# An attention kernel with two mixtures of experts: one attention step moved ahead of another, in one place

## The chip, the cores and the metric

The kernel runs on one core of one Trainium2 chip. What counts is the device time of one execution in microseconds. A core has TensorE (matmuls), VectorE, ScalarE, GpSimd (the profile calls it POOL) and SyncE (SP), which issues most of the DMA transfers. Each engine works through its own instructions in the order in which the program gave them, and waits at an instruction until what it needs is there.

## What is computed

A gated linear attention over 4 batches, 8 heads, 768 tokens and 48 numbers a head, then two layers of experts over the 3072 tokens. The attention keeps a state of 48 by 48 numbers for each head:

```python
for t in range(S):
    state = alpha[:, :, t, :, None] * state + np.einsum('bhd,bhe->bhde', k[:, :, t], v[:, :, t])
    y[:, :, t] = np.einsum('bhd,bhde->bhe', q[:, :, t], state)
```

Its result, 3072 rows of 384, goes through 8 experts, all of them for every row, weighted by a matrix P that is normalised eight times by rows and columns; then through 8 other experts of which each row uses two:

```python
for e in range(E):
    h = np.maximum(x @ w1[e], 0.0)
    ye = h @ w2[e]
    out += P[:, e:e + 1] * ye
```

## The kernel before

The 3072 rows are 24 tiles of 128. The attention works in 24 units, one for each tile, counted from 0 as in the code (a unit is one batch and a stretch of 128 tokens). float32 numbers are split into a float16 upper and a float16 lower half, and a product is made of three float16 products; so most steps have an instruction on ScalarE for the upper half and one on VectorE for the lower half, in that order.

A unit i has these steps, each a function that issues instructions on several engines:

- p1(i): two scans and products with k and q on VectorE (L433 to L438), the halves of v (ScalarE L449, VectorE L450), from unit 4 on products for the state on GpSimd (L444).
- p2(i): TensorE turns k (L457) and multiplies k with q (L467); ScalarE (L459) and VectorE (L460) write the turned k in halves, named `ktok`; ScalarE copies the products (L469) and GpSimd masks them (L470).
- p2b(i): the masked products in halves, named `am`: the upper on ScalarE (L477), the lower on VectorE (L478).
- p3(i): TensorE multiplies `am` with v (L491) and `ktok` with v (L498), VectorE writes the state (L504, later L502), ScalarE the result y (L506).
- p4(i): TensorE turns y (L515), ScalarE writes the upper half `xh` of the tile (L517) and VectorE the lower half `xl` (L518).
- p5(i): small products with the gate weights (L526, L527), their sum on VectorE (L531).

While the attention runs, TensorE is also given work of the first expert, as a stream in a fixed order. `g1t(T, w, j)` is a quarter of the hidden layer for w tiles from tile T on (called a hidden unit below): 18 matmuls from `xh`, `xl` and the split weights (L225), a Relu on ScalarE (L229) and the lower half on VectorE (L230), into `hid`. `g2` is the second layer for one tile: 24 matmuls of 384 columns (L238) and a copy on VectorE (L250). A hidden unit needs `xh` and `xl` of all its tiles.

The order of all this is written by one loop. `order_of(i)` lists which step of which unit comes next in round i: p1 of unit i, p3 of i - 2, p2 and p2b of i - 1, p4 of i - 2, p5 of i - 3. After each step the loop adds a fixed cost for it (`TA`: p1 1.5, p2 2.3, p3 1.6, p4 0.5, p5 0.3) to `t_att`, but only once a tile is available, which is the case from the step after p4 of the first unit on. Then it issues stream items, each with its own cost, until their sum reaches 0.8 of `t_att`. So the place of p4(0) decides from which step on costs are counted.

`W0AT` names the steps after which one of the seven weight pieces of the first expert is split (`w0_step`, ScalarE L150 and VectorE L153): three pieces of 128 x 1024 for the first layer, all of which the first hidden unit needs, and four of 128 x 768. Splitting a piece also issues the load of the piece three further on, on SP. The gate weights are split behind p2(1) (L413, L414).

Of the kernel before, what the change touches and what calls it, by code (L numbers as in the profile page):

```python
# [27 lines left out]
RATIO = 0.8  # L28
FINE = (1, 2, 2, 2)
LATE = 4  # L30
W0AT = (("p1", 2), ("p3", 0), ("p4", 0), ("p5", 0), ("p3", 1), ("p2", 2), ("p4", 1))

WR = 4.0
GW = 1.2
# [4 lines left out]


def order_of(i):
    if i < LATE:
        return ("p1", 0), ("load", -3), ("p3", 2), ("p2", 1), ("p4", 2), ("p2b", 1), ("p5", 3)
    return ("p1", 0), ("load", -3), ("p3", 2), ("p2", 1), ("p2b", 1), ("p4", 2), ("p5", 3)
# [3 lines left out]
def kernel(ctx, tc, q, k, v, alpha, w_gate, w1a, w2a, g2w, n2w, noise, w1b, w2b, out):  # L48
# [485 lines left out]
    def att_units():  # L534
        for i in range(NT + 3):
            for n, d in order_of(i):
                f = dict(p1=p1, load=load, p2=p2, p2b=p2b, p3=p3, p4=p4, p5=p5)[n]
                if 0 <= i - d < NT and (n != "load" or i - d >= NL):
                    yield (lambda f=f, j=i - d: f(j)), n, i - d
# [471 lines left out]
    def w0_step():  # L1011
        i = ws0[0]
        if i < NW:
            w_split(0, i, w0.pop(0))
            if i + 3 < NW:
                w0.append(w0_load(i + 3))
            ws0[0] += 1
# [41 lines left out]
    for u, kind, idx in list(att_units()):  # L1059
        u()  # L1060
        if (kind, idx) in W0AT:
            w0_step()
# [320 lines left out]
```

## Time and profile before

| | us |
|---|---|
| median of 3 runs | 2044.93 (2043.68 to 2045.04) |
| the profiled execution | 2044.31 |
| its span, first to last instruction | 2042.6 |
| TensorE busy | 1982.2 |
| VectorE busy | 1247.5 |
| ScalarE busy | 684.7 |
| GpSimd busy | 605.9 |

The attention fills about the first 241 us of the span, with the first expert's stream in between; then come the other experts of the first layer (to about 1560 us), the routing of the second, and its experts. In the rows below a time is us from the start of the span; in a timeline a row is one instruction or several alike (x22), with its start, its duration, what it writes and reads, and in brackets how long the engine stood idle before it and for what it waited (`DVE am L478` is VectorE's instruction of line 478 that writes `am`). The granted clock of TensorE is given as a share of 2.4 GHz; 0.50 is 1.2 GHz.

### The profile page before, as it was taken

Reading aid. Unit: us, or ns where it says so; the run is one execution under the profiler, and the core shown is the slowest. Engines: PE = TensorE matmul, PEld = TensorE weight load, DVE = VectorE, ACT = ScalarE, POOL = GpSimd, SP = SyncE. Lnnn points to the kernel's source line nnn. Section 1 sums busy time; section 2 is a strip of 40 time slices with the busy share of each in tenths; the row PEclk is TensorE's granted clock in tenths of the full one; section 3 lists DMA queues with packets and bytes.
Section 4 is the critical chain, followed back from the end, with each engine's and each line's share of the span. In section 5 each row is a group of like instructions: output and inputs, shape, how many; then the busy total and the mean of one; then the engine's idle time right before and its main releaser. Section 6 shows DMA issues by size and latency. Waiting matters only on the chain. (4 is left out here: it accounts for less than half of the span.)

```text
span 2042.6 us, 37845 instructions
## 1 busy us (share of the span) xinstructions
PE 1982.2 (97%) x15715; PEld 1335.8 (65%) x15715; DVE 1247.5 (61%) x2642; ACT 684.7 (34%) x1338; POOL 605.9 (30%) x452
## 2 busy tenths in 40 slices
PE   6999999999999999999999999999999899999997
PEld 5888756667667766776677677666555455555554
DVE  8889675666666666566656657554335646454441
ACT  5555422333433343234333323332222323222220
POOL 2434212332332343233324322321000243333322
PEclk9999999999999999999999999999999999999999
DMA  6333010000000000000000001003422458465541
GB/s 218 99 99 118 22 42 32 16 17 22 19 17 30 11 17 27 12 27 16 22 12 24 19 12 42 1 1 96 136 70 66 105 105 191 102 126 133 124 72 24
DMA packets 113565, 119.59 MB, mean 59 GB/s; under 512 B 62692, under 2 KB 95741, under 8 KB 113392
## 3 DMA queue, kind: packets, MB, share of 16 engines
q1 hardware_dynamic: 101968, 97.74, 16.8%
q0 software_dynamic: 11136, 18.89, 5.3%
q8 instruction: 124, 2.03, 0.4%
q10 hardware_dynamic: 288, 0.52, 0.1%
q14 instruction: 49, 0.40, 0.1%
HBM read 85.17 MB, written 21.63 MB: 52 GB/s over the span
## 5 line engine op out<-in xcount | busy, mean ns | idle before, releaser
L285 PE MATMUL bank<-xh,wt 128*128 128x512 f16 x1728 | 520.0, 379 | 1.6 <-DVE acc L248 1.6
L304 POOL TENSOR_TENSOR hid<-ss,hid 128x1024 f16<-128x1024 f32 x144 | 306.8, 2131 | 701.6 <-ACT hid L303 658.4
L319 PE MATMUL long<-wt,hid 128*128 128x192 f16 x6048 | 505.7, 246 | 3.5 <-DVE acc L329 2.6
L319 PEld LDWEIGHTS <-hid 128*128 128x128 f16 x6048 | 500.1, 98 | 12.8 <-issue 3.2
L285 PEld LDWEIGHTS <-wt 128*128 128x128 f16 x2592 | 253.1, 98 | 299.1 <-issue 2.0
L238 PE MATMUL bank<-wt,hid 128*128 128x384 f16 (+1 forms) x2496 | 424.5, 327 | 0.1
L238 PEld LDWEIGHTS <-hid 128*128 128x128 f16 (+1 forms) x2496 | 243.9, 99 | 161.1 <-issue 3.7
L285 PE MATMUL bank<-xl,wt 128*128 128x512 f16 x864 | 327.5, 379 | 0.0
L329 DVE SCALAR_TENSOR_TENSOR acc<-long,Pm,acc 128x192 f32<-128x192 f32 (+1 forms) x360 | 187.4, 533 | 148.3 <-PE long L319 147.7
L308 DVE SCALAR_TENSOR_TENSOR hid<-bank,hid 128x256 f16<-128x256 f32 (+1 forms) x288 | 158.8, 552 | 185.9 <-ACT ss L292 185.9
L308 DVE SCALAR_TENSOR_TENSOR ss<-bank,ss 128x256 f32<-128x256 f32 x576 | 240.5, 420 | 48.2 <-ACT hid L297 31.2
L303 ACT ACTIVATE hid<-ss 128x1024 f16<-128x1024 f32 x144 | 152.2, 1057 | 231.6 <-DVE ss L308 231.6
L291 ACT ACTIVATE hid<-bank 128x256 f16<-128x256 f32 x144 | 53.2, 370 | 408.7 <-PE bank L285 408.7
L153 DVE SCALAR_TENSOR_TENSOR wt<-wst,wt 128x384 f16<-128x384 f32 (+2 forms) x216 | 176.1, 825 | 1.8 <-ACT wt L150 1.8
L891 PEld LDWEIGHTS <-wt 128*128 128x128 f16 x1152 | 112.7, 99 | 90.5 <-issue 4.4
L904 POOL DMA_INDIRECT out_dram<-acc,ix x56 | 91.4, 1632 | 257.0 <-DVE acc L903 238.9
L895 DVE SCALAR_TENSOR_TENSOR hid<-bank,hid 128x384 f16<-128x384 f32 (+1 forms) x128 | 74.2, 588 | 119.5 <-ACT hid L894 119.5
L894 ACT ACTIVATE hid<-bank 128x384 f16<-128x384 f32 (+1 forms) x128 | 65.2, 515 | 221.5 <-PE bank L891 221.5
L150 ACT ACTIVATE wt<-wst 128x384 f16<-128x384 f32 (+2 forms) x216 | 109.7, 535 | 76.5 <-DMA wst<-in_moe_w_dram 76.5
L207 PE MATMUL bank<-xh,wt 128*128 128x512 f16 x384 | 121.8, 379 | 0.7 <-DVE acc L329 0.7
L891 PE MATMUL bank<-xl,wt 128*128 128x384 f16 (+1 forms) x576 | 106.5, 342 | 0.0
L891 PE MATMUL bank<-xh,wt 128*128 128x384 f16 (+1 forms) x576 | 106.3, 342 | 0.0
(187 smaller groups left out, 1676.1 us busy)
## 6 DMA issues: line engine op xcount, KB each, us to landing
wst<-in_moe_w_dram SPq DMA_DIRECT2D x38, 512.0 KB, 3.4
wst<-in_moe_w_dram SPq DMA_DIRECT2D x46, 384.0 KB, 3.2
acc<-in_moe_w_dram SPq DMA_DIRECT2D x18, 384.0 KB, 4.6
la<-in_alpha_dram SPq DMA_DIRECT2D x24, 260.0 KB, 2.7
lk<-in_k_dram SPq DMA_DIRECT2D x24, 256.0 KB, 3.0
wt<-in_q_dram SPq DMA_DIRECT2D x22, 256.0 KB, 3.9
acc<-in_moe_w_dram SPq DMA_DIRECT2D x10, 512.0 KB, 7.1
out_dram<-zero SPq DMA_DIRECT2D x6, 768.0 KB, 4.7
```

The source lines that it names most:

```text
L150: nc.scalar.activation(hi, src, AF.Copy, scale=SW)
L153: nc.vector.scalar_tensor_tensor(lo, src, SW, hi, op0=OP.mult, op1=OP.subtract)
L207: nc.tensor.matmul(p, w1s(e, a, kc, f), x[:, kc, s], start=(n == 0), stop=(n == 3 * KC - 1))
L238: nc.tensor.matmul(p, h(a, f, s), w2s(x, b, f), start=(f + n == 0), stop=(f == FC - 1 and n == 2))
L285: nc.tensor.matmul(p, w1s(e, a, kc, f), x[:, kc, tok], start=(n == 0), stop=(n == 3 * KC - 1))
L303: nc.scalar.activation(lefts(e, nb, j, 0, S1, 4), sums, AF.Copy)
L304: nc.gpsimd.tensor_sub(lefts(e, nb, j, 1, S1, 4), sums, lefts(e, nb, j, 0, S1, 4))
L308: nc.vector.scalar_tensor_tensor(out, p, 0.0, x, op0=OP.max, op1=op)
L319: nc.tensor.matmul(out, left(e, nb, j, a, aop)[:, q * 128:(q + 1) * 128], w2t(e, b, wop, j), start=start and n == 0, stop=stop and n == 3 ...
L329: nc.vector.scalar_tensor_tensor(a, p, Pm[:, T, e:e + 1], a, op0=OP.mult, op1=OP.add)
L891: nc.tensor.matmul(p, w1s(x, a, kc, f), xt[:, b * KC + kc, :], start=(i == 0), stop=(i == 3 * KC - 1))
L904: d = nc.gpsimd.indirect_dma_start(out=out, out_offset=bass.IndirectOffsetOnAxis(ap=ix, axis=0), in_=y, in_offset=None, bounds_check=N - 1 ...
```

## The change

In round 2 alone p4(0) is issued ahead of p2(1) in place of behind it. The weight pieces 1 and 2 are split behind p4(0) and p2(1), which before were split behind p3(0) and p4(0); pieces 3 to 6 keep their steps. Nothing else is edited, and no work is added or removed; two new lines shift the line numbers behind them by 2.

```diff
--- before.py
+++ after.py
@@ -28,7 +28,7 @@
 RATIO = 0.8
 FINE = (1, 2, 2, 2)
 LATE = 4
-W0AT = (("p1", 2), ("p3", 0), ("p4", 0), ("p5", 0), ("p3", 1), ("p2", 2), ("p4", 1))
+W0AT = (("p1", 2), ("p4", 0), ("p2", 1), ("p5", 0), ("p3", 1), ("p2", 2), ("p4", 1))
 
 WR = 4.0
 GW = 1.2
@@ -39,6 +39,8 @@
 
 
 def order_of(i):
+    if i == 2:
+        return ("p1", 0), ("load", -3), ("p3", 2), ("p4", 2), ("p2", 1), ("p2b", 1), ("p5", 3)
     if i < LATE:
         return ("p1", 0), ("load", -3), ("p3", 2), ("p2", 1), ("p4", 2), ("p2b", 1), ("p5", 3)
     return ("p1", 0), ("load", -3), ("p3", 2), ("p2", 1), ("p2b", 1), ("p4", 2), ("p5", 3)
```

What the loop makes of it reaches further: a tile counts as available one step earlier, p2(1)'s cost of 2.3 is counted, and from there to the end of the attention the stream items stand some 1.8 (0.8 of 2.3) earlier in the order. 54 items are issued by the end of the attention, 53 before. The order of SP's transfers is the same.

VectorE, at the start, from the copy of unit 0's state on; before:

```order
L504 COPY acc<-bank 128x384
L153 SCALAR_TENSOR_TENSOR wt_72<-acc,wt_72 128x1024
L460 SCALAR_TENSOR_TENSOR ktok<-bank,ktok 128x512
L413 TENSOR_SCALAR wg_111<-wg 128x3x8
L414 SCALAR_TENSOR_TENSOR wg_111<-wg,wg_111 128x3x8
L518 TENSOR_TENSOR xl<-bank,xh 128x3x128
L153 SCALAR_TENSOR_TENSOR wt_72<-acc,wt_72 128x1024
L478 TENSOR_TENSOR am<-acc,am 128x1024
L433 SCALAR_TENSOR_TENSOR ce_119<-la_83,inv 128x520
```

and now:

```order
L506 COPY acc<-bank 128x384
L520 TENSOR_TENSOR xl<-bank,xh 128x3x128
L155 SCALAR_TENSOR_TENSOR wt_72<-acc,wt_72 128x1024
L462 SCALAR_TENSOR_TENSOR ktok<-bank,ktok 128x512
L155 SCALAR_TENSOR_TENSOR wt_72<-acc,wt_72 128x1024
L415 TENSOR_SCALAR wg_111<-wg 128x3x8
L416 SCALAR_TENSOR_TENSOR wg_111<-wg,wg_111 128x3x8
L232 SCALAR_TENSOR_TENSOR hid<-bank,hid 128x2x128 x2
L480 TENSOR_TENSOR am<-acc,am 128x1024
L435 SCALAR_TENSOR_TENSOR ce_119<-la_83,inv 128x520
L437 TENSOR_TENSOR ks<-lk_80,ce_119 128x512
```

`xl` of tile 0 (L518, now L520) has moved up past a weight piece, `ktok` and the gate weights (`wg`); the lower halves of the first two hidden units (L232, `hid`) now stand ahead of `am` of unit 1 (L478, now L480) and so ahead of p1(3), which begins with the `ce` row; before they stood behind p1(3).

VectorE, at units 2 and 3, behind p1(4); before:

```order
L230 SCALAR_TENSOR_TENSOR hid<-bank,hid 128x2x128
L504 COPY acc<-bank 128x384
L230 SCALAR_TENSOR_TENSOR hid<-bank,hid 128x2x128
L460 SCALAR_TENSOR_TENSOR ktok<-bank,ktok 128x512
L250 COPY acc<-bank 128x384
L478 TENSOR_TENSOR am<-acc,am 128x1024
L518 TENSOR_TENSOR xl<-bank,xh 128x3x128
```

and now:

```order
L232 SCALAR_TENSOR_TENSOR hid<-bank,hid 128x2x128
L252 COPY acc<-bank 128x384
L506 COPY acc<-bank 128x384
L462 SCALAR_TENSOR_TENSOR ktok<-bank,ktok 128x512
L480 TENSOR_TENSOR am<-acc,am 128x1024
L520 TENSOR_TENSOR xl<-bank,xh 128x3x128
```

The copy of the first `g2` (L250, now L252) has moved ahead of p3(2)'s state copy (L504, now L506) and of `ktok` of unit 3: TensorE now makes this `g2` ahead of p3(2) and p2(3), and before behind p2(3). The hidden units of tile 2 follow p2(3), p4(2) and p5(1) directly.

ScalarE, at unit 6, from `ktok` of unit 6 on; before:

```order
L459 ACTIVATE ktok<-bank 128x512
L469 ACTIVATE acc<-bank 128x512 x2
L229 ACTIVATE hid<-bank 128x2x128
L477 ACTIVATE am<-acc 128x1024
L517 ACTIVATE xh<-bank 128x3x128
L530 ACTIVATE pr<-bank 128x8
L449 ACTIVATE vh<-hid 128x384
L506 ACTIVATE y<-bank 128x384
L459 ACTIVATE ktok<-bank 128x512
```

and now:

```order
L461 ACTIVATE ktok<-bank 128x512
L471 ACTIVATE acc<-bank 128x512 x2
L479 ACTIVATE am<-acc 128x1024
L519 ACTIVATE xh<-bank 128x3x128
L532 ACTIVATE pr<-bank 128x8
L451 ACTIVATE vh<-hid 128x384
L231 ACTIVATE hid<-bank 128x2x256
L508 ACTIVATE y<-bank 128x384
```

Between p2(6) and p3(6) (the `y` row) there now stands the first hidden unit of two tiles, 4 and 5 (`hid` 128x2x256), behind `am` of unit 6 and `xh` of tile 5; before, a hidden unit of tile 3 stood there (and a `g2`), ahead of `am`.

## Rows read from the trace of the kernel before

**Rows 1.** The page, busy time of each engine: us, share of the span, instructions.

```profile
PE 1982.2 (97%) x15715; PEld 1335.8 (65%) x15715; DVE 1247.5 (61%) x2642; ACT 684.7 (34%) x1338; POOL 605.9 (30%) x452
```

**Rows 2.** Stages: PE, PEld, DVE, ACT, POOL busy us (instructions), clock, DMA share, GB/s.

```profile
16.00:36.00 20.00, 14.30 (x189) 12.71 (x190) 19.28 (x30) 12.18 (x22) 4.14 (x4) 0.83 0.71 239
...
51.00:241.00 190.00, 181.24 (x2233) 152.24 (x2231) 166.83 (x253) 96.07 (x189) 73.70 (x78) 1.00 0.27 85
241.00:1560.00 1319.00, 1312.47 (x10134) 888.90 (x10131) 807.71 (x1684) 435.85 (x845) 370.29 (x239) 1.00 0.10 31
```

**Rows 3.** Timeline, TensorE, first units: start, us, engine, line, operation, count, wait.

```profile
18.23 1.08 PE L457 MATMUL bank<-ident,ks 128*128 128x128 f32 x4
...
22.01 0.22 PE L225 MATMUL bank<-xh,wt 128*128 128x128 f16 x1 [1.07 <-ACT xh L517]
25.01 0.27 PE L225 MATMUL bank<-xl,wt 128*128 128x128 f16 x1 [2.78 <-DVE xl L518]
...
26.14 0.40 PE L225 MATMUL bank<-xh,wt 128*128 128x128 f16 x2 [0.23 <-DVE wt L153]
...
29.11 0.97 PE L491 MATMUL bank<-vh,am 128*128 128x48 f16 x24
...
36.82 0.22 PE L225 MATMUL bank<-xl,wt 128*128 128x128 f16 x1 [0.92 <-DVE xl L518]
```

**Rows 4.** Timeline, VectorE, the same stretch.

```profile
24.87 1.21 DVE L153 SCALAR_TENSOR_TENSOR wt<-acc,wt 128x1024 f16<-128x1024 f32 x1
26.00 1.22 DVE L478 TENSOR_TENSOR am<-acc,am 128x1024 f16<-128x1024 f32 x1
27.14 1.23 DVE L433 TENSOR_TENSOR_SCAN ce<-la,inv 128x520 f32<-128x520 f32 x1
...
31.57 0.74 DVE L230 SCALAR_TENSOR_TENSOR hid<-bank,hid 128x256 f16<-128x256 f32 x2
...
35.01 0.96 DVE L153 SCALAR_TENSOR_TENSOR wt<-acc,wt 128x768 f16<-128x768 f32 x1 [0.43 <-ACT wt L150]
...
36.22 0.55 DVE L518 TENSOR_TENSOR xl<-bank,xh 128x384 f16<-128x384 f32 x1
```

**Rows 5.** Timeline, ScalarE, the same stretch.

```profile
17.51 0.49 ACT L506 ACTIVATE y<-bank 128x384 f32<-128x384 f32 x1 [1.05 <-PE bank L491]
...
24.11 1.06 ACT L477 ACTIVATE am<-acc 128x1024 f16<-128x1024 f32 x1 [1.21 <-POOL acc L470]
...
29.35 0.38 ACT L229 ACTIVATE hid<-bank 128x256 f16<-128x256 f32 x1 [1.54 <-PE bank L225]
```

**Rows 6.** TensorE by windows of 1 us: busy (instructions), granted clock, DMA share, GB/s.

```profile
22.00:23.00 1.00, 0.22 (x1) 0.90 1.04 397
...
29.00:30.00 1.00, 1.00 (x29) 0.68 0.00 0
...
1575.00:1576.00 1.00, 0.04 (x1) 0.94 0.00 0
...
1579.00:1580.00 1.00, 1.00 (x6) 0.86 0.12 22
```

**Rows 7.** Timeline, all engines, from the eighth unit's k, q products on.

```profile
93.52 1.16 PE L467 MATMUL bank<-qs,ks 48*128 48x128 f32 x16
...
97.78 1.23 DVE L478 TENSOR_TENSOR am<-acc,am 128x1024 f16<-128x1024 f32 x1 [2.49 <-ACT am L477]
...
98.92 0.55 DVE L518 TENSOR_TENSOR xl<-bank,xh 128x384 f16<-128x384 f32 x1
...
99.06 0.70 PE L491 MATMUL bank<-vh,am 128*128 128x48 f16 x21 [0.88 <-DVE am L478]
```

**Rows 8.** TensorE's waits between 30 and 245 us: total, times, longest.

```profile
PE bank L491 <- DVE am L478: 10.0, 16, 1.3
...
PE bank L515 <- ACT y L506: 0.6, 1, 0.6
```

**Rows 9.** Timeline, TensorE, one of these waits (unit 6).

```profile
79.53 0.72 PE L491 MATMUL bank<-vh,am 128*128 128x48 f16 x22 [0.31 <-DVE am L478]
```


## Prediction

> **What bounds the kernel now.** I count units, tiles and weight pieces from 0, as the code does; line numbers are those of before. The page first: TensorE is busy for 1982.2 of 2042.6 us [rows 1], so the whole can only move by what it stands idle, or runs slowly, in one stage. The table of stages says where: it stands idle for 8.8 of 190 us between 51 and 241 us, for 6.5 of 1319 us after that, and for 5.7 of 20 us between 16 and 36 us [rows 2]. The edit lies in that last stretch, and VectorE is busy there for 19.3 of 20 us: an engine that works through its queue without a pause sets the pace, not TensorE, whose holes are its waits. The timelines name them: 2.78 us for the lower half xl of tile 0, later 0.92 us for xl of tile 1 [rows 3], both written by VectorE's L518. Further on the wait that returns is p3's for `am`, 10.0 us in 16 pieces [rows 8]. What follows the attention is TensorE's own work with 0.5% of holes; a lateness at 241 us is not made good there, since its waits hang on work that moves with it.
>
> **The first lateness.** What is wanted works: y of unit 0 is there at 18.00 (17.51 + 0.49) [rows 5], TensorE is free at 18.23 [rows 3], p4's three transposes take some 0.8 (four took 1.08), and p2(1) starts 0.8 later, for which nobody waits. On VectorE xl of tile 0 now stands ahead of weight piece 1 (1.1 us, as piece 2 takes from 24.87 to 26.00 [rows 4]), the k copy and the gate weights, about 2.0 us of work: TensorE sees it at 23.0 in place of 25.01 [rows 3]. But the first hidden unit also needs the lower half of weight piece 2. Ahead of it VectorE has the same work as before less the gate weights' 0.3, so it starts at 24.57 in place of 24.87 and ends at 25.8 [rows 4]; "one item later" costs the pieces nothing, and gains 0.3. The last 27 matmuls of the pair follow at the spacing of before, 2.97 us for 28 of them (26.14 to 29.11) [rows 3], so ScalarE's Relu of the second unit starts at 29.05 in place of 29.35 [rows 5].
>
> Now the price. The pair of hidden units is issued ahead of p2b(1), so both Relus stand ahead of am(1) on ScalarE, and both L230 ahead of L478 on VectorE. Before, am(1) went at 24.11 on ScalarE and 26.00 on VectorE while TensorE still worked on the pair [rows 4, 5]. Now it waits for the pair: ScalarE about 29.35 to 30.4, VectorE at 30.4, 4.4 us later. Queued behind L478 is all of p1(3), which started at 27.14 and now starts at about 31.55; the two L230 that stood behind it are done already (0.7), and VectorE's one wait in this stretch, 0.43 at 35.01 for a weight piece [rows 4], goes, since ScalarE will be ahead there. Its xl of tile 1 (36.22) is late by 4.4 - 0.7 - 0.4 = 3.3 us, and TensorE's matmul that waited for it (36.82) [rows 3] comes at about 40.1 with the same work done up to there. **+3.3** (1.8 if the pair runs at the upper clock, whose 27 matmuls take 1.4 less; 3.7 if the 0.4 is not regained). SP's order is unchanged: its loads for unit 6 wait for p1(3) and go some 4 us later, needed over 20 us after that; the sixth weight piece behind them goes as late as its split.
>
> **The slots after it.** An attention step now counts p2(1)'s 2.3 in the pacing, and every stream item after it stands 1.8 us of work (about two small items) earlier in the order. What matters is how much TensorE has between p2(i) and what needs am(i) or xl(i-1): call that slot i. Slot 8 shows the chain at its shortest, with VectorE waiting: the k, q products start at 93.52, p3's third matmul at 99.06, and TensorE stood 0.88 of these 5.54 us [rows 7]. It had one two-tile hidden unit in between: 18 matmuls of twice the columns, 36 x 0.053 (half of 2.97 / 28) = 1.9 us. So a slot with nothing but p4 and p5 costs 0.88 + 1.9 = 2.8. Where a hidden unit that needs the newest xl comes first it is worse: L518 ends at 98.92 + 0.55 [rows 7], seen 0.05 later, 6.0 us after the products' start; 1.1 of them are products, 0.5 p4 and p5, 0.1 a first matmul: it costs 4.3. Five slots are of these kinds in the new order:
>
> - Slot 3: the first g2 now stands ahead of p3(2) and p2(3), no longer behind p2(3); hidden units of tile 2 come next. 4.3 for the longest wait of before, 1.3 [rows 8]: **+3.0**.
> - Slot 6: the first two-tile unit, of tiles 4 and 5, needs xl of tile 5, which stands behind am(6). 4.3 for 0.31 [rows 9]: **+4.0**.
> - Slot 10: the same for tiles 8 and 9, with one two-tile unit as cover: 4.3 - 1.9 = 2.4 for nothing: **+2.4**.
> - Slots 13 and 23: only p4 and p5. 2.8 each, for 0.3 each of before (like the one in rows 9) and the wait of 0.6 for the last y [rows 8], ahead of which a hidden unit now stands: **+4.4**.
> - The others: of the 10.0 [rows 8], slot 3's 1.3 and three pieces of 0.31 are replaced above; 7.8 are left. In the new order three slots (15, 18, 21) have one two-tile unit, 0.88 each, and some ten have more, 0.3 each: 5.6. **-2.2**, bounds -5 and +3, since in-order waits behind a late g2 copy may add to them.
>
> **The clock.** The granted clock fell to 1.2 GHz at 22.8 and came back at 29.64 (0.90 of 22 to 23, 0.68 of 29 to 30), and after a stand of TensorE it fell again at 1575.9 for 3.4 us [rows 6]. 3.4 us at half speed cost up to 1.7. The stands before 40 us and in slots 3, 6, 13 and 23 are as long or longer, so I expect five new falls, 0 to 8.5 us. Where the slowed work covers the next chain it is free, so I take 1.0 each: **+5**. The fall at 22.8 stays, since TensorE still waits for weight piece 2.
>
> **Sum.** 3.3 + 3.0 + 4.0 + 2.4 + 4.4 - 2.2 + 5 = +19.9 us. The profiled execution took 2044.31 us (span 2042.6), so 2064.2; the median before lies 0.6 above it: 2064.8, 1.0% more.
>
> **Rivals.** *Only the start is late.* The first lateness and slot 3 are read from engines' queues that I can follow; from slot 4 on the new interleaving may be as good as the old, since VectorE has 23 of 190 us free there [rows 2] and a long stand lets it run ahead of the next waits. Then 3.3 + 3.0 = 6.3: 2051.2. Against it: the chain of rows 7 was measured with VectorE idle, so a free VectorE does not shorten it. *Faster.* TensorE's hole, not VectorE's queue, decides up to 40 us: the first xl comes 2.0 us sooner, the four hidden units of tile 0 stand as 72 matmuls in a row in place of 36, 18 and 18, and the clock does not fall, which at 2.3 us lost of the 4.6 between 25.01 and 29.64 gives 4.3 in all: 2040.6. It decides if am(1) is not needed before 33 us, that is if p1(3) behind it has that much slack. The Trainium skill, "TensorE: Matmul & The Clock Gate", section "Loop structure matters more than you think", says that matmuls kept back to back keep the engine's clock up and waits between them lower it; by that rule alone the change is a gain of this size. Rows 6 bear out that waits lower it, but here the row of 72 stands behind the same weight piece as the 36 did. Against this rival is VectorE's 19.3 of 20 us [rows 2]. *No change:* the lateness of 3.3 is regained in later waits, 10.0 us in all [rows 8], and the new holes are filled: 2041 to 2049.
>
> **How the numbers follow.** About 0.2% (4.1 us) is what a measurement of this kernel can tell from no change. The forecast, 2057 to 2076, 0.62; only the start late, 2049 to 2057, 0.18; within 0.2%, 0.09; faster, 0.06; above 2076 0.05 (eight or ten more slots at 0.88, or every fall of the clock at full price). So slower 0.85, same 0.09, faster 0.06. The range 2050 to 2076 leaves out about 2 in 10.
>
> **What would show it.** In the new trace VectorE's L478 of unit 1 stands behind two L230 and starts near 30.4, with VectorE idle for some 3.5 us between 26 and 30.4; the first xl ends near 22.9; TensorE's wait for xl of tile 1 lasts about 3 us and ends near 40; waits of 4 us for xl near 56 and 90, of 2.8 for am in slots 13 and 23, and short windows of half clock after them. TensorE's idle time up to 245 us grows by about 15. If am(1) starts before 28, or the hidden unit of tile 5 finds its xl ready, the forecast is wrong.

## The result, and the profile after

| | before | after |
|---|---|---|
| median, us (lowest to highest, runs) | 2044.31 (2043.15 to 2045.04, 4) | 2069.57 (2068.40 to 2070.42, 4) |
| the profiled execution | 2044.31 | 2069.13 |
| its span | 2042.6 | 2067.4 |
| TensorE busy in it | 1982.2 | 1991.8 |

The changed kernel takes 1.0124 times as long (95% interval 1.0111 to 1.0137): 25.3 us more, where 19.9 more was forecast. Line numbers of after are those of before plus 2.

The page of after, its span, the busy time of each engine [rows 1] and the granted clock in 40 slices:

```profile
span 2067.4 us, 37847 instructions
...
PE 1991.8 (96%) x15715; PEld 1342.5 (65%) x15715; DVE 1248.6 (60%) x2642; ACT 685.2 (33%) x1338; POOL 602.6 (29%) x452
...
PEclk8999999999999999999999999999999999999999
```

The span grew by 24.8 us. TensorE is busy for 9.6 more of them with the same 15715 matmuls, and stands idle for the other 15.2 (2067.4 - 1991.8 = 75.6, for 2042.6 - 1982.2 = 60.4). So there are two losses, of idle time and of clock. The idle time is in the attention. TensorE's waits there (total, times, longest; for [rows 8]):

```profile
PE bank L227 <- ACT xh L519: 9.1, 4, 2.9
PE bank L227 <- DVE xl L520: 6.8, 4, 3.5
PE bank L493 <- DVE am L480: 6.6, 10, 1.0
PE bank L493 <- ACT am L479: 3.2, 3, 1.5
PE bank L529 <- DVE xl L520: 0.6, 1, 0.6
PE bank L528 <- ACT xh L519: 0.6, 1, 0.6
```

They make 26.9 us. Before they were 12.6: 10.0 for `am` and 0.6 for y [rows 8], and 2.0 for `xh` and `xl` of tile 1, 0.92 of which is the last of [rows 3]. The wait for `am` has become 9.8 in fewer and partly longer pieces. What is new is the hidden unit that waits for a tile just written: 15.9 us for `xh` and `xl` in four places.

VectorE at the start (start, duration, line, what is written and read, idle time before it and its cause; for [rows 4]):

```profile
27.73 0.42 DVE L232 SCALAR_TENSOR_TENSOR hid<-bank,hid 128x256 f16<-128x256 f32 x1 [1.46 <-ACT hid L231]
29.66 0.42 DVE L232 SCALAR_TENSOR_TENSOR hid<-bank,hid 128x256 f16<-128x256 f32 x1 [1.50 <-ACT hid L231]
30.60 1.23 DVE L480 TENSOR_TENSOR am<-acc,am 128x1024 f16<-128x1024 f32 x1 [0.52 <-ACT am L479]
31.74 1.23 DVE L435 TENSOR_TENSOR_SCAN ce<-la,inv 128x520 f32<-128x520 f32 x1
...
35.71 0.99 DVE L452 SCALAR_TENSOR_TENSOR vh<-wt,vh 128x384 f16<-128x384 f32 x1
...
40.09 0.55 DVE L520 TENSOR_TENSOR xl<-bank,xh 128x384 f16<-128x384 f32 x1
```

The engine that had no pause before stands for 3.48 us (1.46 + 1.50 + 0.52) in front of L480, which starts 4.60 later than before, behind the pair of hidden units. The queue behind it is late with it, and ends in `xl` of tile 1, 3.87 us late.

TensorE, the long waits in order of time (for [rows 3, 9]):

```profile
22.90 0.22 PE L227 MATMUL bank<-xl,wt 128*128 128x128 f16 x1 [1.49 <-DVE xl L520]
...
36.95 0.22 PE L227 MATMUL bank<-xh,wt 128*128 128x128 f16 x1 [1.80 <-ACT xh L519]
...
40.68 0.27 PE L227 MATMUL bank<-xl,wt 128*128 128x128 f16 x1 [3.52 <-DVE xl L520]
...
56.74 0.22 PE L227 MATMUL bank<-xh,wt 128*128 128x128 f16 x1 [2.90 <-ACT xh L519]
58.08 0.27 PE L227 MATMUL bank<-xl,wt 128*128 128x128 f16 x1 [1.13 <-DVE xl L520]
...
90.87 0.27 PE L227 MATMUL bank<-xh,wt 128*128 128x256 f16 x1 [2.89 <-ACT xh L519]
92.22 0.37 PE L227 MATMUL bank<-xl,wt 128*128 128x256 f16 x1 [1.08 <-DVE xl L520]
...
132.25 0.27 PE L227 MATMUL bank<-xh,wt 128*128 128x256 f16 x1 [1.55 <-ACT xh L519]
133.59 0.37 PE L227 MATMUL bank<-xl,wt 128*128 128x256 f16 x1 [1.08 <-DVE xl L520]
...
165.64 0.22 PE L493 MATMUL bank<-vh,am 128*128 128x48 f16 x2 [1.55 <-ACT am L479]
166.90 0.91 PE L493 MATMUL bank<-vh,am 128*128 128x48 f16 x22 [1.04 <-DVE am L480]
```

A stand is in two parts each time: for the upper half from ScalarE, then, after one or two matmuls, for the lower half from VectorE. From 56 us on these are slots 3, 6, 10 and 13; slot 23 is like 13, near 262 us.

The clock after one of these stands, TensorE in windows of 1 us (busy, instructions, granted clock, DMA share, GB/s; for [rows 6]):

```profile
58.00:59.00 1.00, 0.92 (x10) 0.50 0.00 0
...
61.00:62.00 1.00, 1.00 (x27) 0.81 0.00 0
```

Half of full speed is 1.2 GHz. Added up over all windows of 1 us from 18 to 275 us, the granted clock is at 1.2 GHz for 6.8 us before, in one piece (from 22.8 on), and for 30.7 us after: 6.8 at the start as before, another 6.8 from 37.5 on, and 3.4 each near 58, 92, 133, 167 and 263.

### The profile page after: what moved, and what is told of

Same layout as the page of the kernel before. It is cut to its first block, busy times and chain, and to the rows that moved or that the text cites. A ratio compares the mean times of both kernels' runs of the same rounds, so it can differ in the third digit from the quotient of the medians.

```text
span 2067.4 us, 37847 instructions
## 1 busy us (share of the span) xinstructions
PE 1991.8 (96%) x15715; PEld 1342.5 (65%) x15715; DVE 1248.6 (60%) x2642; ACT 685.2 (33%) x1338; POOL 602.6 (29%) x452
## 5 line engine op out<-in xcount | busy, mean ns | idle before, releaser
L287 PE MATMUL bank<-xh,wt 128*128 128x512 f16 x1728 | 520.0, 379 | 2.2 <-DVE acc L250 2.2
L287 PEld LDWEIGHTS <-wt 128*128 128x128 f16 x2592 | 253.2, 98 | 299.6 <-issue 2.6
L240 PE MATMUL bank<-wt,hid 128*128 128x384 f16 (+1 forms) x2496 | 423.2, 326 | 0.0
L240 PEld LDWEIGHTS <-hid 128*128 128x128 f16 (+1 forms) x2496 | 243.5, 99 | 160.0 <-issue 2.5
L287 PE MATMUL bank<-xl,wt 128*128 128x512 f16 x864 | 327.5, 379 | 0.0
```

The source lines that it names most:

```text
L240: nc.tensor.matmul(p, h(a, f, s), w2s(x, b, f), start=(f + n == 0), stop=(f == FC - 1 and n == 2))
L287: nc.tensor.matmul(p, w1s(e, a, kc, f), x[:, kc, tok], start=(n == 0), stop=(n == 3 * KC - 1))
```

## The experiments

The kernel before ran on the same chip beside each: its median was 2043.40 us beside e1 to e4, 2044.21 beside e5 to e8, 2044.24 beside the last two. A ratio is against that run. After itself gave 25.3 us more than before.

| run | what it is | median, us | ratio (95%) |
|---|---|---|---|
| e1 | after, p2(1) not counted | 2044.45 | 1.0008 (0.9999 to 1.0018) |
| e2 | before, 2.3 more counted | 2066.72 | 1.0112 (1.0097 to 1.0128) |
| e3 | after, first items behind p1(3) | 2066.62 | 1.0114 (1.0098 to 1.0129) |
| e4 | before with the new `W0AT` | 2044.59 | 1.0003 (0.9994 to 1.0013) |
| e5 | after, long stands filled | 2061.27 | 1.0089 (1.0072 to 1.0106) |
| e6_shift050 | e1, 0.5 more counted | 2046.61 | 1.0013 (1.0003 to 1.0023) |
| e7_shift075 | e1, 0.75 more counted | 2058.05 | 1.0071 (1.0054 to 1.0087) |
| e8_pair_ahead | e1, one pair ahead of am(1) | 2048.11 | 1.0021 (1.0011 to 1.0030) |
| e9_hold_p3 | e1, nothing issued behind p3 | 2042.42 | 0.9989 (0.9980 to 0.9998) |
| e10_even | e9, counted anew from unit 6 on | 2038.66 | 0.9980 (0.9971 to 0.9989) |

The theory: the loss is not in what the change moves, but in what the loop counts for it. p4(0) ahead of p2(1) makes a tile available one step sooner, so 2.3 more is counted, and the whole stream stands earlier among the attention steps. The rivals: the late start alone; the moved steps or weight pieces themselves; and, for the size, idle time alone without the clock.

**e1: the moved steps without the count.**

```diff
-        avail = nxt
+        avail = -1 if (kind, idx) == ("p2", 1) else nxt
```

> p4(0) ahead of p2(1) and the weight pieces as in the changed kernel, but a tile counts as available from p2b(1) on, as before, so the stream stands where it stood. Theory (the place of the stream items is the cost): 2044.5 us, within 2 us of before; the first xl seen near 23.0, xl of tile 1 near 36.5 to 36.9, no new waits. Rival (turning y ahead of the k, q products is the cost): 2048 to 2052. Rival (the hole at 22 to 25 us was worth its length): 2040 to 2042.

Measured: the time of before, as far as the noise allows (the interval ends at 0.18% more). All moved steps are where the change puts them, and they show no cost; they gain nothing either. TensorE in e1, its timeline:

```profile
20.04 2.08 PE L469 MATMUL bank<-qs,ks 48*128 48x128 f32 x16
...
23.13 0.26 PE L227 MATMUL bank<-xl,wt 128*128 128x128 f16 x1 [0.79 <-DVE xl L520]
...
26.61 0.42 PE L227 MATMUL bank<-xh,wt 128*128 128x128 f16 x2
...
30.48 0.27 PE L227 MATMUL bank<-xh,wt 128*128 128x128 f16 x2
...
31.91 1.16 PE L469 MATMUL bank<-qs,ks 48*128 48x128 f32 x16
...
36.94 0.22 PE L227 MATMUL bank<-xl,wt 128*128 128x128 f16 x1 [1.11 <-DVE xl L520]
```

and TensorE in e1 in a long window (busy, instructions, granted clock, DMA share, GB/s):

```profile
18.00:26.00 8.00, 5.43 (x39) 1.00 0.91 302
```

The stand of 2.78 us [rows 3] is 0.79. The granted clock of 1.00 in this window must not be taken for full speed. The first record of the clock in this trace is a rise at 29.2, and the view shows 1.00 where it has no record. The matmuls tell more: two of 128 columns take 0.42 us up to 29 and 0.27 after, and the 16 products of a p2 take 2.08 at 20.04 and 1.16 at 31.91. So TensorE ran at 1.2 GHz up to about 29 us here too. Yet `xl` of tile 1 is seen at 36.94, before at 36.82 [rows 3]: VectorE is busy for 20.65 of the 21 us from 16 to 37, writes `xl` when its queue has come to it, and what TensorE saves earlier it waits there. So the "faster" rival had the hole right, and its gain is not there. Its clock did not come about in this execution; that a higher one would only have lengthened the wait for `xl` follows from VectorE's queue and was not run.

**e2: the count without the moved steps.**

```diff
-            t_att += TA[kind]
+            t_att += TA[kind] + (TA["p2"] if (kind, idx) == ("p2b", 1) else 0.0)
```

> The kernel before, its order of steps and pieces, but p2(1)'s cost of 2.3 is counted in the pacing, at p2b(1): the stream stands 1.8 us of items earlier, as in the changed kernel, and p4(0) stays behind p2(1). Theory: the slots 3, 6, 10, 13, 23 cost what they cost in the changed kernel; the first pair of hidden units stands behind am(1) but ahead of p1(3), so the first lateness is about 2 in place of 3.3 to 3.9: 2066 to 2069 us. Rival (the place of p4(0) is the cause): 2044 to 2047.

Measured: 23.3 of the 25.3 us. TensorE's waits in e2 (lines of before):

```profile
PE bank L225 <- ACT xh L517: 9.1, 4, 2.9
...
PE bank L225 <- DVE xl L518: 5.5, 4, 2.2
```

The wait for `xh` is that of after to the tenth. Only the longest wait for `xl` is shorter, 2.2 for 3.5. With e1 this settles the cause: the count alone makes nearly all of it, and without the count nothing clear of noise is left.

**e3: the count, but no stream item ahead of p1(3).** What is due behind p2(1) and p2b(1) is issued behind p1(3); so am(1) and the scans don't wait for the hidden units.

```diff
-            while t_g < RATIO * t_att:
+            while t_g < RATIO * t_att and (kind, idx) not in (("p2", 1), ("p2b", 1)):
```

> The changed kernel, but the stream is held until p1(3) is issued, so am(1) and p1(3) stand ahead of the first pair; from there on the stream stands as in the changed kernel. Theory: the first lateness (3.3 to 3.9) and the fall of the clock before 40 us (up to 1.7) go, the five slots stay: 2064.5 us (2062 to 2066.5). Rival (the later waits follow from the late start): 2046 to 2052.

Measured: 3.0 us less than after between the medians (2066.62 against 2069.57), 2.0 less when each is taken against its own before (23.2 and 25.3 more); it lies 0.1 above the range expected. The first lateness is mostly gone, in VectorE's timeline of e3:

```profile
26.08 1.22 DVE L480 TENSOR_TENSOR am<-acc,am 128x1024 f16<-128x1024 f32 x1
```

and in TensorE's:

```profile
36.72 0.22 PE L227 MATMUL bank<-xh,wt 128*128 128x128 f16 x1 [1.80 <-ACT xh L519]
37.80 0.27 PE L227 MATMUL bank<-xl,wt 128*128 128x128 f16 x1 [0.86 <-DVE xl L520]
```

The later waits are unchanged (9.1 for `xh`, 6.6 and 3.2 for `am`). So the rival "only the start is late" falls: without the late start the kernel is still 1.14% slower.

**e4: the weight pieces alone.** The kernel before with the new `W0AT`.

> The kernel before, only the two weight pieces split one item later. Theory: VectorE does the same work ahead of the third piece, so no more than 0.6 us either way: 2044 to 2045.5 us. Rival (the later pieces hold up the first hidden unit): 2047 or more.

Measured: no difference.

**e5: the clock.** After, with matmuls that nobody needs put into the long stands (their results are overwritten), so that the clock stays up while the waits remain. `fill` issues so many matmuls of 256 columns, in the hidden units of the tiles and in the steps p3 that are named (`fill` itself and its two calls are left out here).

```diff
+FILL = {1: 44, 2: 32, 4: 32, 8: 19}
+FILL3 = {13: 18, 23: 18}
```

> The changed kernel, with matmuls on data that is long there put into TensorE's stands, whose results are overwritten: 44 of 256 columns ahead of the first hidden unit of tile 1 (stand 5.3 us), 32 ahead of those of tiles 2 and 4 (4.0), 19 ahead of that of tile 8 (2.6), 18 ahead of p3(13) and of p3(23) (2.6, 2.5). The waits stay, the clock need not fall. Theory (the falls cost 1.7 each and are not covered): the 20 us of half clock that the changed kernel has more than before go, and 7 to 9 us with them: 2061 to 2063. Rival (work slowed by the clock would have waited anyway): 2067 to 2070.

Measured: 8.3 us less than after (2061.27 against 2069.57). TensorE in e5, in long windows:

```profile
18.00:31.00 13.00, 9.69 (x85) 0.76 0.57 201
31.00:51.00 20.00, 20.00 (x280) 0.99 0.30 86
51.00:241.00 190.00, 182.23 (x2254) 1.00 0.28 89
```

The clock is at 1.2 GHz for 6.8 us in all, as before, and only at the start. The other 17.1 us remain, with TensorE kept busy by work that brings nothing. So some 8 of the 25 us are the clock's, and 17 the waits'. (Some 0.4 of the 8 are another thing: the split of v that takes 0.99 us at 35.71 in after takes 0.55 here.)

**e6 and e7: how the loss grows with the count.** e1 with 0.5 or 0.75 more counted at p2b(1), with nothing issued there.

```diff
+            t_att += TA[kind] + (0.5 if (kind, idx) == ("p2b", 1) else 0.0)
+            while t_g < RATIO * t_att and (kind, idx) != ("p2b", 1):
```

> Steps as in the changed kernel, pacing as before but with 0.5 in place of the 2.3 counted ahead of p1(3). By the length of the chain (5.54 us for am, 6.0 for xl from the k, q products on) and what stands in each slot of this order, no slot is short of cover that was not before, two more have 0.9 of wait: 2044.5 to 2047 us. Rival (any shift of the stream against the steps costs): in proportion to the changed kernel, 0.5 / 2.3 of 22, 2049.

> The same with 0.75 in place of 0.5. By the same reckoning the first g2 moves ahead of p2(3) and slots 18 and 23 lose their g2: stands of 3 to 4 us in slot 3 and of 2.8 in 18 and 23, 9 us of idle more than before, and three falls of the clock at 1.7: 2055 to 2059 us. Rival (in proportion): 2051.

Measured: 2.4 us more than before for 0.5 (its runs spread from 2043.33 to 2048.98), 13.8 for 0.75, both in the ranges expected from slots counted in the new order; a loss in proportion to the count (2051 for 0.75) is ruled out. Slot 3 shows what happens. TensorE in e6 and then in e7, from the products of p2(3) on (L469; L240 is the first g2):

```profile
42.66 1.16 PE L469 MATMUL bank<-qs,ks 48*128 48x128 f32 x16
43.76 4.07 PE L240 MATMUL bank<-wt,hid 128*128 128x384 f16 x24
...
49.71 0.72 PE L493 MATMUL bank<-vh,am 128*128 128x48 f16 x22 [1.36 <-DVE am L480]
```

```profile
44.57 4.06 PE L240 MATMUL bank<-wt,hid 128*128 128x384 f16 x24
...
49.00 1.16 PE L469 MATMUL bank<-qs,ks 48*128 48x128 f32 x16
...
53.29 0.22 PE L493 MATMUL bank<-vh,am 128*128 128x48 f16 x2 [2.52 <-ACT am L479]
54.55 1.03 PE L493 MATMUL bank<-vh,am 128*128 128x48 f16 x22 [1.04 <-DVE am L480]
```

With 0.25 more in the count the g2 of 4 us goes ahead of the products: the slot loses its whole cover, and its wait goes from 1.36 to 3.56 us (2.52 + 1.04). A stream item is inside a slot or it is not.

**e8: the pair ahead of am(1), and then the old count.** After, with the 2.3 taken off again once the first items are issued behind p2(1).

```diff
+            if (kind, idx) == ("p2", 1):
+                t_att -= TA[kind]
```

> As the first kernel of the study (steps of the changed kernel, stream as before), but the first two hidden units are issued ahead of p2b(1), as in the changed kernel, and nothing behind them moves. Theory: only the first lateness, 3.3 us, and the fall of the clock that the longer stand before 40 us brings (up to 1.7): 2047.5 to 2050. Rival (later waits take it up): 2044 to 2046.

Measured: 3.9 us more than before, 2.8 more than e1 (each against its own chip's before). TensorE in e8:

```profile
30.65 0.22 PE L493 MATMUL bank<-vh,am 128*128 128x48 f16 x2 [1.42 <-ACT am L479]
31.91 0.72 PE L493 MATMUL bank<-vh,am 128*128 128x48 f16 x22 [1.04 <-DVE am L480]
...
40.97 0.22 PE L227 MATMUL bank<-xl,wt 128*128 128x128 f16 x1 [0.92 <-DVE xl L520]
```

`xl` of tile 1 is seen 4.1 us later than before (40.97 for 36.82 [rows 3]), after a wait as short as that of before: TensorE's own stands for am(1) and a fall of the clock behind them (1.2 GHz for 3.4 us, from 33 us on) have made it as late as VectorE. The late start by itself costs 3 to 4 us here (2 to 3 by e3), and nothing of it comes back in the attention: the first L287, behind the same 3035 matmuls, starts at 314.3, in before (L285) at 310.0.

**e9 and e10: the same rule used forward.** If what stands in a slot decides, items that the loop issues behind p3 (outside the slots) are worth more behind the next p2. e9 is e1 with that:

```diff
+            while t_g < RATIO * t_att and not (kind == "p3" and idx >= 3):
```

e10 takes 1.4 off the count at p1(6), once, and counts 2.5% more from there on, so that the two-tile units fall into the slots one by one (`late` starts as False):

```diff
+            if (kind, idx) == ("p1", 6):
+                late = True
+                t_att -= 1.4
+            t_att += TA[kind] * (1.025 if late else 1.0)
```

> Steps as in the changed kernel, stream as before, but from p3(3) on no stream item is issued straight behind p3(i); it goes behind p2(i + 1) instead, into the slot where TensorE waits. Theory (slots need about 3.5 us of TensorE work behind the k, q products): by the reckoning of the chain five of the seven waits of 0.9 and most of the shorter ones go: 2039 to 2042 us. Rival (VectorE, busy for 88% of this stretch, delays am instead): 2043 to 2046.

> As the one before, and from p1(6) on the stream is 1.1 us of items later and 2.5% denser, so that by the same reckoning every slot has its cover. Theory: another 1 to 2 us less: 2037.5 to 2041 us. Rival (VectorE delays am instead, or the stream runs short at the end): 2042 to 2046.

Measured: e9 is 1.8 us faster than before between the medians, 0.4 short of the range expected; e10 is 5.6 us faster between the medians, 0.20% (0.11 to 0.29%) by the ratio, with runs from 2037.07 to 2043.12. It beats both kernels. TensorE's waits in e10 between 31 and 275 us:

```profile
PE bank L493 <- DVE am L480: 4.9, 9, 1.3
PE bank L227 <- ACT xh L519: 1.1, 1, 1.1
PE bank L227 <- DVE xl L520: 0.9, 1, 0.9
PE bank L517 <- ACT y L508: 0.6, 1, 0.6
```

The wait for `am` is 4.9 in 9 pieces, for 10.0 in 16 [rows 8]. These 5.1 us are nearly the whole gain.

## Why the prediction was right

The time, 2069.57, lies 4.8 above the one forecast and inside the range, and it came the way that was forecast. Step by step, the waits from the timeline of after:

| term | forecast, us | measured, us |
|---|---|---|
| first lateness | +3.3 | +3.9 (`xl` of tile 1 at 40.68 for 36.82) |
| slot 3 | 4.3 for 1.3: +3.0 | 2.90 + 1.13 for 1.3: +2.7 |
| slot 6 | 4.3 for 0.31: +4.0 | 2.89 + 1.08 for 0.31: +3.7 |
| slot 10 | +2.4 | 1.55 + 1.08: +2.6 |
| slots 13, 23 | +4.4 | 5.1 for 1.2: +3.9 |
| the others | 5.6 for 7.8: -2.2 | 4.8 for 7.8: -3.0 |
| not foreseen: p5(23) waits for the last `xh`, `xl` | | +1.2 |
| idle time | +14.9 | +15.0 by these rows, +15.2 over the span |
| clock | +5 | +9.6 over the span, +10.7 up to the first L287 |

- **First lateness.** The first `xl` was to be seen at 23.0 and is at 22.90. L480 was to start at 30.4 and starts at 30.60; VectorE was to stand for 3.5 us and stands for 3.48. Two L232 less behind it give back 0.7, as worked out. The 0.43 for a weight piece is gone too, but the split of v (L452) takes 0.99 where it took 0.55, which eats it: 4.60 - 0.7 = 3.9, above the bound of 3.7 that was set for just this case. Of these 3.9 only 2.9 are idle time of TensorE (22.0 up to 40.68, 19.1 up to 36.82 before); the other 1.0 is matmuls at 1.2 GHz.
- **Slots.** All five were named rightly, and their sizes are within 0.3 us. The chain of rows 7 holds with VectorE free (it stands idle for 2.08, 2.43 and 2.79 us ahead of `am` in slots 3, 6 and 13): what is not in the slot is stood. The form differs: the stand is first for `xh` (2.9) and then for `xl` (1.1), not one wait for `xl`. That the sum of the idle terms comes out within 0.1 is partly luck: the rows miss by +0.6, -0.3, -0.3, +0.2, -0.5, -0.8 and +1.2.
- **The clock** is the term that was mis-sized. Five new falls at 1.0 were taken; there are six up to 275 us (slot 10 brings the one not foreseen), one of them twice as long: 23.9 us at 1.2 GHz more. Up to the first L287 (335.8 us; L285 in before, 310.0), behind the same 3035 matmuls, TensorE is busy for 289.4 us in place of 278.7. So these falls cost 10.7, or 1.5 for 3.4 us, not 1.0; by e5 it is 8.3, or 1.2. Full price would have been 11.9 (23.9 / 2): that the slowed work would be partly free, as cover of the next chain, was argued and hardly holds. Over the whole span it is 9.6, since the fall at 1575.9 of before [rows 6] does not come in after; the prediction did not count on that.
- **Rivals.** "Only the start is late" falls with e3. "No change" falls: the late start came back in no later wait (e8). "Faster" falls with e1, by the reason given against it, VectorE's full queue. The rule named beside it (the Trainium skill, "TensorE: Matmul & The Clock Gate", section "Loop structure matters more than you think") is borne out as to the clock by after and e5: six new falls come with the new stands, and none of the six with the stands filled. The gain that it promised here did not come, 2044.45 against 2043.40; as TensorE was at 1.2 GHz up to 29 us in the trace of e1, and from some 24 to 30 in those of after and the other runs with the moved steps, no trace shows them with the clock up there.
- **At no cost.** That the earlier p4(0) and the weight pieces one item later cost nothing clear of noise by themselves is shown by e1 and e4.

## What to carry to other kernels

Where one loop mixes two streams by counted costs, a step that is moved past the point where counting starts shifts everything behind it; write out, for each wait of the old trace, what the waiting engine now has between the start of the chain and its end, and the difference is the price. A hole whose end is set by another engine's full queue is not worth its length, and filling it early may put that engine's urgent work behind. Add to each new stand of some microseconds the work that runs at half clock after it, at most of the full price (8.3 to 10.7 of 11.9 here). Read the clock from the matmuls' own durations as well as from its record.

## What the runs showed of the hardware that was not expected

- **Stands cut in two.** The clock fell in the second part of a stand that one or two matmuls divide, or just behind it: at 133.05 with parts of 1.55 and 1.08 us, at 167.19 with 1.55 and 1.04, in e3 at 37.21 with 1.80 and 0.86. The stands alone do not decide it: parts of 1.1 and 0.9, for `xh` and `xl` of tile 1, brought a fall near 37 or 38 in the traces of e4, e9 and e10, and none in those of before and e6. The fall at 22.8 of before begins 0.6 us into the stand of 2.78 [rows 3], so it does not follow from that stand's length. After 0.55 (at 123.43) or 0.88 (at 247.34) alone none was seen.
- **A fall longer than the others.** Falls last 3.4 us near 58, 92, 133, 167 and 263, and 6.8 in the first 45 us of after (two of two) and of before (one of one); the second one lasts 6.8 in e2 too, and 3.4 in e3, e4 and e7 to e10. What decides between the two stays open.
- **The split of v.** For unit 3 it took 0.99 us in after, at 35.71, beside GpSimd's mask, which took longer too; in before, e1, e2, e3 and e8, where the two don't overlap, it took 0.55. This is no single case: of the 24 splits in before 12 take 0.98, each beside the mask for at least 0.57 us, and 12 take 0.54 to 0.55, 11 of them beside nothing on GpSimd and one beside the mask for 0.26. GpSimd's timeline of after:

```profile
35.36 1.83 POOL L472 TENSOR_SCALAR_AFFINE_SELECT acc<-acc 128x512 f32<-128x512 f32 x2 [12.20 <-ACT acc L471]
```

and of before:

```profile
33.83 1.22 POOL L470 TENSOR_SCALAR_AFFINE_SELECT acc<-acc 128x512 f32<-128x512 f32 x2 [9.75 <-ACT acc L469]
```

That each slows the other is a reading of these rows and counts; no run here was made to show it.
